# A scan-attention and gated-MLP kernel on one Trainium2 core: another start-up, and eight shared slots for raw weights and splits

## The chip, the cores and the metric

The kernel runs on one core of a Trainium2 chip. Five engines run side by side, each with its own instruction stream in order: TensorE (PE, matmuls from SBUF into PSUM), VectorE (DVE), ScalarE (ACT), GpSimd (POOL) and SyncE (SP, which here only issues DMAs). They meet through semaphores. The metric is the device time of one execution in microseconds; the median of several executions counts.

## The reference

Two stages. The first is a chunked linear recurrence over a sequence of 768 for 4 batches and 8 heads (head size 32, state size 16), the second a gated MLP over the 3072 resulting tokens (256 wide, 1536 hidden). Both are computed in float32.

```python
log_a = np.log(np.clip(a, 1e-06, 1.0))
for c in range(nc):
    ...
    cum = np.cumsum(la, axis=-1)
    L = np.exp(cum[:, :, :, None] - cum[:, :, None, :])
    L = L * causal
    CB = np.einsum('bhin,bhjn->bhij', Cc, Bc)
    y_intra = np.einsum('bhij,bhjd->bhid', CB * L, xc)
    y_inter = np.einsum('bhin,bhnd->bhid', Cc, state) * decay_to_i[:, :, :, None]
    ...
    state = decay_full[:, :, None, None] * state + np.sum(Bx, axis=2)

g = x @ w_gate
silu = g * (1.0 / (1.0 + np.exp(-g)))
return (silu * (x @ w_val) @ w_out).astype(np.float32)
```

## The kernel before

The sequence is cut into six blocks (`k` = 0 to 5) of 128 positions for all batches, and each block into two pieces of 64 (`Q`). A block goes through the attention stage and then through the MLP.

**Attention of a block.** The decays are running products of the clipped `a`. `L` holds, for each pair of positions, the product of the decays between them: DVE scans it (`scan_j`, one scan of 520 elements a batch) over a tile in which each row of `a` is repeated on 64 partitions, with `dj` (a repeated unit matrix) marking where each product starts. `E` holds the decays from a piece's start in the layout of the states, scanned with `dn`. The matmuls are `scores` (tile `S`, from `C` with the heads apart, `Cz`, and `B`), `sums` (tile `st`, the new states from x and the weighted B), `values` (tile `y`, from x and `L` after DVE's `mix` multiplied `S` into it) and `carried` (added into `y`, from `C` times `E` and the state `T`). `apart` masks `st` into `T`, on ACT or DVE; `step` carries the state from piece to piece. `weigh_b` (written into `xb`) and `weigh_c` (written into `bc`) apply the decays to B and C.

For blocks 1 to 5 the decays come from a clipped copy in DRAM: `all` is loaded (two DMAs), clipped by `clip_all` on DVE, and written to `clipped`; `load_aj` and `load_an` then read it with repetition over partitions. Block 0 has its own way in: for three batches (`SPREAD = 3`) eight rows of `a` (`rows`, clipped by `clip_rows`) are spread over 128 partitions by a matmul with a selection matrix `pick`, in two halves of 260 columns (tiles `a`), and scanned out of PSUM; the fourth batch and `E` are loaded with repetition by DMA, clipped and scanned in SBUF.

**MLP of a block.** For each of 12 slices `f` of the hidden size, `gate_val` computes gate and value (tiles `gv`, two matmul groups), `silu` (ACT) and `product` (DVE) give `sg`, `hid_high` and `hid_low` split `sg` into two float32r halves `hh` and `hl`, and `project` adds three float32r matmuls per output half into `po`. From block 1 on, gate and value are also three float32r products of split operands; block 0 uses float32 matmuls on x as it is (`xf`), since the split weights are not ready.

**Weights.** The 18 weight tiles (12 `wg`, 6 `wo`) are passed as 64-bit words, and each is fetched (`w_fetch`, 512 KB, tile `wg0r` and so on in pool `raw`) and brought to float32 in steps on ACT and DVE (`w_magnitude`, `w_range`, `w_rest`, `w_shift`, `w_sign`, `w_round`, the last shown as CUSTOM_DVE_ANT_0 on `wg0w`), then split (`w_high`, `w_low`). A raw slot is free after `w_round`. There are four.

**Order.** Nothing is issued where the code names it. Each step is added to a `Plan` (line 43) with its engines, an estimated cost, a rank (due time), what it needs, which slots it takes and what it uses; `Plan.order` (line 114) picks again and again the step that can start first, by rank, and so fixes each engine's stream. `Ordered` (line 184) keeps the streams in that order. A wait in a stream holds up all that stands behind it there. `idle` adds filler matmuls (tile `rest`, 128 columns of ones times 384) in two groups given by `IDLE` (line 851). `LATE` holds some loads back until a certain weight has been fetched.

Of the kernel before, what the change touches and what calls it, by code (L numbers as in the profile page):

```python
# [19 lines left out]
P = 128  # L20
# [10 lines left out]
HB = 4  # L31

# [10 lines left out]
class Plan:  # L43
# [49 lines left out]
    def chain(self, e, order):  # L93

        steps = {op.gives: op for op in self.ops if e in op.engines}
        for g, h in zip(order, order[1:]):
            steps[h].needs += (("issued", g),)
        for g, op in steps.items():
            if g not in order:
                op.needs += (("issued", order[-1]),)  # L100
        self.marked = {steps[g]: ("issued", g) for g in order}
# [12 lines left out]
    def order(self):  # L114
# [14 lines left out]
        while len(out) < len(self.ops):  # L129
# [31 lines left out]
            given = [(op.gives, end), (self.marked.get(op), self.clock[e])]  # L161
# [41 lines left out]
def scan_moe_kernel(ctx: ExitStack, tc, aj, an, bc, xb, wgv, wo, cst, sel, out):  # L203
# [13 lines left out]
    raw = pool("raw", 4)  # L217
# [23 lines left out]
    def load_rows():  # L241

        t = moe.tile([K * BATCH, 2, T + 32], F32, tag="xl", name="rows")
        t = bl[0]["rows"] = t[:, 0, : H * W]
        sp.dma_start(t, aj[0].rearrange("q (b c) -> (q b) c", b=BATCH))

    def load_first_aj():

        t, c = bl[0]["L"][:, H * SPREAD :], SPREAD * H * W
        for q in range(K):  # L250
            sp.dma_start(
                t[piece(q)].rearrange("p g t -> p (g t)"),
                aj[0, q, c:].unsqueeze(0).to_broadcast([Q, BATCH * H * W - c]),
            )

    def load_first_an():
        sp.dma_start(
            bl[0]["E"].rearrange("p b q t -> p (b q t)"),
            an[0].unsqueeze(1).to_broadcast([H, N, BATCH * K * W]),
        )  # L260
# [45 lines left out]
    def clip_all():  # L306
        clip(bl[0]["all"].rearrange("p i a t -> p (i a) t")[:, :, 1:])

    def clip_j(b):
        clip(bl[0]["L"][:, H * b : H * b + H, 1:])  # L310

    def clip_n():
        clip(bl[0]["E"].rearrange("p b q t -> p (b q) t")[:, :, 1:])
# [5 lines left out]
    def clip_rows():  # L319
        clip(bl[0]["rows"].rearrange("p (g t) -> p g t", t=W)[:, :, 1:])  # L320
# [334 lines left out]
    load_first_aj()  # L655
    load_first_an()
# [3 lines left out]
    def do(f, *a):  # L660
# [4 lines left out]
        dict(mm=4, at=4, L=1, E=1, bc=1, xb=1, Cz=1, T=2, raw=4, w=1, x=2, hh=HB, sg=SG, ob=2),  # L665
        dict(SP=3.0, Act=3.0, DVE=1.0, PE=1.5, Pool=2.0, Page=0.0, **{"-": 0.7}),
# [3 lines left out]
    GV, PO, ATT, FIRST, PACE0 = 2.82, 1.41, 5.0, 18.0, 3.5  # L670
# [16 lines left out]
    add("DVE", 0.6, lambda: ve.tensor_copy(dj, eye.unsqueeze(1).to_broadcast([P, H, W])), -8.5, ["cs"], gives="dj")  # L687
# [25 lines left out]

    add("SP", 0.96, load_all, -6, gives="all", lag=1.5)
    add("DVE", 0.3, clip_all, 3.0, ["all"], gives="clipped")
    add("SP", 0.48, write_all, -6, ["clipped"], gives="written", lag=1.5)


    for k in range(NB):
# [10 lines left out]
        q = ("SP", 0.48) if k else ("-", 0.0)  # L730

# [175 lines left out]
```

## Time and profile before

| what | us |
|---|---|
| median of 3 runs | 367.49 (365.65 to 367.71) |
| the profiled execution, its own time | 365.92 |
| its span, first to last instruction | 364.1 |
| PE busy / DVE busy / ACT busy | 354.8 / 233.4 / 127.2 |
| first gate/value matmul of block 0 | 23.20 |
| last output matmul done, the chain's end on PE | 360.9 |

A row of a timeline gives start, length, engine, line, operation, output and inputs (partitions x elements) and a count; neighbours of one kind are merged. In brackets stands the idle time ahead of the row and what ended it. A row of the chain of waits gives start, length and what the end of the program hung on during that time. A row of grouped DMA issues gives the count, the size of one and the time from issue to landing. "SPq" is SyncE's queue. All compute lines are L192, the helper that records every operation, so tiles tell the rows apart.

### The profile page before, as it was taken

To read this page: it belongs to the slowest core of one execution; us is meant where nothing else is said; L and a number is where in the kernel's file an instruction comes from. 1 tells how busy PE (TensorE), PEld (TensorE's weight loads), DVE (VectorE), ACT (ScalarE), POOL (GpSimd) and SP (SyncE) were. 2 spreads that over 40 slices of the span, in tenths; PEclk is the share of its full clock that TensorE was granted. 3 is DMA by queue.
4 is the path that set the end of the run, shared out by engine and by line. 5 is a ranking of instruction groups with operands and counts; after the bars stand their busy time and mean duration, and the time that the engine had idled before them with its cause. 6 is when DMAs were issued, how large, how long until landed. Compare 5 with 4: busy or idle time off the path is not lost.

```text
span 364.1 us, 7409 instructions
## 1 busy us (share of the span) xinstructions
PE 354.8 (97%) x3199; PEld 267.6 (73%) x3199; DVE 233.4 (64%) x430; ACT 127.2 (35%) x223; POOL 0.8 (0%) x6
## 2 busy tenths in 40 slices
PE   8989799999999999999999999999999999999996
PEld 4544345578886788878788878788888788888895
DVE  3997899998999579547166947158755153343250
ACT  3454674543423463322133322133221133321242
POOL 0000000000000000000000000000000000000000
PEclk9999999999999999999999999999999999999999
DMA  7669552484100065100048100036100000100001
GB/s 221 246 205 205 194 175 75 169 206 132 59 0 4 2 194 156 58 0 4 2 119 174 59 0 4 2 121 171 59 2 2 2 2 0 58 2 0 0 2 58
DMA packets 8736, 28.60 MB, mean 79 GB/s; under 512 B 1008, under 2 KB 1912, under 8 KB 8064
## 3 DMA queue, kind: packets, MB, share of 16 engines
q1 hardware_dynamic: 8416, 26.82, 25.2%
q10 hardware_dynamic: 288, 1.31, 0.9%
q8 instruction: 25, 0.41, 0.5%
q14 instruction: 7, 0.06, 0.0%
HBM read 24.79 MB, written 3.35 MB: 77 GB/s over the span
## 4 chain that ended last, share of the span: by engine, by line
PE 85%; DMA 5%; DVE 5%; ACT 1%; issue 1%; SPq 1%; DVEq 0%; ACTq 0%
PE gv L192 51%; PE po L192 27%; PE y L192 4%; DMA L<-clipped 4%; DMA L<-in_aj 2%; PE S L192 2%; DVE L L192 1%; PE rest L192 1%; PE st L192 1%; DVE sg L192 1%; SPq L192 1%; DVE wg0w L192 0%; DVE wo4w L192 0%; DVE wo3w L192 0%; ACT sg L192 0%
## 5 line engine op out<-in xcount | busy, mean ns | idle before, releaser
L192 DVE TENSOR_TENSOR sg<-gv,sg 128x512 f32<-128x512 f32 x72 | 49.5, 687 | 78.1 <-PE gv L192 77.9
L192 ACT ACTIVATE sg<-gv 128x512 f32<-128x512 f32 x72 | 43.0, 597 | 112.9 <-PE gv L192 112.8
L192 DVE TENSOR_TENSOR hl<-sg,hh 128x512 fp32r<-128x512 f32 x72 | 49.2, 688 | 22.2 <-ACT hh L192 21.6
L192 ACT CAST hh<-sg 128x512 fp32r<-128x512 f32 x54 | 33.6, 622 | 44.2 <-PE po L192 25.5
L192 DVE TENSOR_TENSOR_SCAN L<-L,dj 128x520 f32<-128x520 f32 x21 | 25.4, 1230 | 4.3 <-DMA L<-clipped 4.3
L192 DVE TENSOR_TENSOR L<-S,L 128x512 f32<-128x512 f32 x24 | 15.4, 682 | 1.9 <-PE S L192 1.9
L192 ACT COPY ob<-po 128x512 f32<-128x512 f32 (+1 forms) x13 | 7.2, 555 | 21.1 <-PE po L192 20.6
L192 PE MATMUL rest<-unit 128*128 128x384 bf16 x47 | 12.7, 421 | 1.1 <-DVE warm L192 1.1
L192 PEld LDWEIGHTS y<-L,xb 64*32 64x32 f32 x768 | 8.4, 105 | 4.7 <-issue 3.6
L192 PEld LDWEIGHTS <-unit 128*128 128x128 bf16 x47 | 5.3, 120 | 7.7 <-issue 5.7
L192 PE MATMUL y<-L,xb 64*32 64x64 f32 x768 | 10.4, 224 | 0.0
L192 PE MATMUL po<-hh,wo0h 128*128 128x512 f32 (+1 forms) x26 | 10.3, 395 | 0.0
L192 PE MATMUL po<-hh,wo2h 128*128 128x512 f32 (+1 forms) x26 | 9.8, 378 | 0.0
L192 PE MATMUL po<-hh,wo3h 128*128 128x512 f32 (+1 forms) x26 | 9.8, 377 | 0.0
L192 PE MATMUL po<-hh,wo5h 128*128 128x512 f32 (+1 forms) x26 | 9.8, 377 | 0.0
L192 PE MATMUL po<-hl,wo0h 128*128 128x512 f32 (+1 forms) x26 | 9.7, 375 | 0.0
L192 PE MATMUL po<-hh,wo0l 128*128 128x512 f32 (+1 forms) x26 | 9.7, 374 | 0.0
L192 PE MATMUL po<-hh,wo1h 128*128 128x512 f32 (+1 forms) x26 | 9.7, 373 | 0.0
L192 PE MATMUL po<-hl,wo2h 128*128 128x512 f32 (+1 forms) x26 | 9.7, 373 | 0.0
L192 PE MATMUL po<-hl,wo3h 128*128 128x512 f32 (+1 forms) x26 | 9.7, 373 | 0.0
L192 PE MATMUL po<-hh,wo4h 128*128 128x512 f32 (+1 forms) x26 | 9.7, 373 | 0.0
L192 PE MATMUL po<-hl,wo4h 128*128 128x512 f32 (+1 forms) x26 | 9.7, 373 | 0.0
(285 smaller groups left out, 778.9 us busy)
## 6 DMA issues: line engine op xcount, KB each, us to landing
L<-clipped SPq DMA_DIRECT2D x10, 520.0 KB
xb<-in_xb SPq DMA_DIRECT2D x5, 768.0 KB
out<-ob SPq DMA_DIRECT2D x11, 256.0 KB, 2.2
bc<-in_bc SPq DMA_DIRECT2D x5, 512.0 KB
E<-clipped SPq DMA_DIRECT2D x5, 260.0 KB
xb<-in_xb ACTq DMA_DIRECT2D x1, 768.0 KB, 5.9
bc<-in_bc ACTq DMA_DIRECT2D x1, 512.0 KB
wg0r<-in_wgv SPq DMA_DIRECT2D x1, 512.0 KB
```

The costliest lines, as they stand in the source:

```text
L192: ins = getattr(self.engine, name)(*a, **k)
```

## The change

What it does:

- All four batches of block 0's `L` and its `E` are spread by TensorE from `rows`, which now holds eight rows of `aj` and eight of `an`; `pick` has five selection matrices. `load_first_aj`, `load_first_an`, `clip_j` and `clip_n` are gone. `E` is scanned out of PSUM in two halves, by an order written out after the four mixes.
- `cs` is loaded first on ACT's queue; SP begins with the two loads of `rows` and `pick`, then the two of `all`. `dj` may be copied by ACT.
- `clip_all` runs on GpSimd and is ranked early. The weights wg2 to wg6 and block 1's `bc` and `xb` need `clipped` or `written`; the weights are fetched in their order.
- Pool `raw` has eight slots. `hh` and `hl` of a slice are halves of one tile from the same pool, where before each had four slots of its own.
- `chain`, which tied one engine to an order, becomes `follow`, which ties a list of steps whichever engine they run on; three lists are followed.
- `IDLE` has three groups of eight: at the start, after the scores of block 0, and after its carried values. `unit` is three times as wide, so that a filler reads it without repetition.
- Some estimated costs, lags and ranks of the planner change; `apart` of block 0 is given to ACT.

```diff
+RAW = 8
-    def chain(self, e, order):
-        steps = {op.gives: op for op in self.ops if e in op.engines}
+    def follow(self, order):
+        steps = {op.gives: op for op in self.ops}
         for g, h in zip(order, order[1:]):
             steps[h].needs += (("issued", g),)
...
-    raw = pool("raw", 4)
+    raw = pool("raw", RAW)
...
-    unit = const.tile([P, P], BF16, name="unit")
-    pick = const.tile([K * BATCH, SPREAD, P], F32, name="pick")
+    unit = const.tile([P, 3 * P], BF16, name="unit")
+    pick = const.tile([H, BATCH + 1, P], F32, name="pick")
...
     def load_rows():
-        t = moe.tile([K * BATCH, 2, T + 32], F32, tag="xl", name="rows")
-        t = bl[0]["rows"] = t[:, 0, : H * W]
-        sp.dma_start(t, aj[0].rearrange("q (b c) -> (q b) c", b=BATCH))
-    def load_first_aj():
...
-    def load_first_an():
...
+        t = moe.tile([H, 2, T + 32], F32, tag="xl", name="rows")
+        t = bl[0]["rows"] = t[:, :, : H * W]
+        sp.dma_start(t[:, 0], aj[0].rearrange("q (b c) -> (q b) c", b=BATCH))
+        sp.dma_start(t[:, 1], an[0])
...
     def clip_all():
-        clip(bl[0]["all"].rearrange("p i a t -> p (i a) t")[:, :, 1:])
+        t = bl[0]["all"].rearrange("p i a t -> p (i a) t")[:, :, 1:]
+        ge.tensor_scalar(t, t, 1e-6, 1.0, ALU.max, ALU.min)
...
     def scan_spread(b, i):
+        if b < BATCH:
+            to, d = bl[0]["L"][:, H * b : H * b + H].rearrange("p g t -> p (g t)"), dj
+        else:
+            to, d = bl[0]["E"].rearrange("p b q t -> p (b q t)"), dn
...
     def hid_high(k, f, e):
         t = hid[k, f]
-        for n in ("hh", "hl"):
-            t[n] = moe.tile([P, T], F32R, tag=n, name=f"{n}{k}_{f}", bufs=HB)
+        pair = raw.tile([P, 2, T], F32R, tag="wraw", name=f"hh{k}_{f}")
+        t["hh"], t["hl"] = pair[:, 0], pair[:, 1]
         copy(e, t["hh"], t["sg"])
...
     load_rows()
+    se.dma_start(cs, cst)
     sp.dma_start(pick, sel)
-    sp.dma_start(cs, cst)
...
-        add("SP", 0.48, do(w_fetch, i), r - 9.0, takes=[("raw", ("raw", i))], gives=("raw", i), lag=1.75)
+        add("SP", 0.48, do(w_fetch, i), r - 9.0, ["clipped"] if 2 <= i < 7 else [("y", 0)] if i == 7 else [], takes=[("raw", ("raw", i))], gives=("raw", i), lag=2.1)
...
-    add("SP", 0.96, load_all, -6, gives="all", lag=1.5)
-    add("DVE", 0.3, clip_all, 3.0, ["all"], gives="clipped")
-    add("SP", 0.48, write_all, -6, ["clipped"], gives="written", lag=1.5)
+    add("SP", 0.96, load_all, -9, gives="all", lag=0.9)
+    add("Pool", 1.0, clip_all, -9, ["all"], gives="clipped")
+    add("SP", 0.48, write_all, -9, ["clipped"], gives="written", lag=0.9)
...
+    halves = [(b, i) for b in range(BATCH) for i in range(2)]
+    plan.follow([
+        *(("spread", b, i) for b, i in halves), *(("S", 0, b) for b in range(BATCH)),
+        *(("spread", BATCH, i) for i in range(2)), *(("st", 0, b) for b in range(BATCH)), ("idle", 1, 0),
+    ])
+    plan.follow([("raw", i) for i in range(NW)])
+    plan.follow([("L", 0, b) if i else ("scan0", b) for b, i in halves] + [("M", 0, p) for p in range(NP)] + [("scan0", BATCH), ("E", 0), ("ce", 0)])
...
-SPREAD = 3
-IDLE = [-9.0] * 8 + [-3.8, -3.3, -2.8] + [-1.2 + 0.1 * i for i in range(12)], [15.0 + 0.5 * i for i in range(24)]
+IDLE = [-9.0] * 8, [-1.2 + 0.1 * i for i in range(8)], [0.5 + 0.5 * i for i in range(8)]
+IDLE_AFTER = [], [("S", 0, BATCH - 1)], [("y", 0)]
+FETCH = dict(aj=10.0, an=29.0, bc=12.0, xb=31.0)
```

The streams that come out of it, at three places. First SP, from the first weight on; names carry the block or weight number and then a buffer number. Before:

```order
L192 DMA wg0r_124<-in_wgv 128x1024
L192 DMA wg1r_129<-in_wgv 128x1024
L192 DMA wg2r_133<-in_wgv 128x1024
L192 DMA wg3r_140<-in_wgv 128x1024
L192 DMA clipped_85<-all_114 128x2x195
L192 DMA bc1_356<-in_bc 128x1024
L192 DMA xb1_366<-in_xb 128x1536
L192 DMA wg4r_381<-in_wgv 128x1024
L192 DMA L1_359<-clipped_85 64x2080 x2
L192 DMA E1_360<-clipped_85 128x1x520
L192 DMA wg5r_403<-in_wgv 128x1024
L192 DMA wg6r_418<-in_wgv 128x1024
```

And now, from the same weight on:

```order
L190 DMA wg0r_115<-in_wgv 128x1024
L190 DMA wg1r_121<-in_wgv 128x1024
L190 DMA clipped_85<-all_108 128x2x195
L190 DMA wg2r_210<-in_wgv 128x1024
L190 DMA wg3r_231<-in_wgv 128x1024
L190 DMA wg4r_233<-in_wgv 128x1024
L190 DMA wg5r_272<-in_wgv 128x1024
L190 DMA wg6r_275<-in_wgv 128x1024
L190 DMA bc1_363<-in_bc 128x1024
L190 DMA L1_365<-clipped_85 64x2080 x2
L190 DMA E1_366<-clipped_85 128x1x520
L190 DMA wg7r_390<-in_wgv 128x1024
```

The write of `clipped` moved ahead of wg2, and wg4 to wg6 moved ahead of all loads of block 1; `xb1` went behind wg7.

On PE, at the first gate/value tiles of block 0 (`gv0`, slice, gate or value), there stood before:

```order
L192 MATMUL gv0_0_0_383<-xf_119,wg0w_259 128x512 x2
L192 MATMUL gv0_0_1_400<-xf_119,wg0w_259 128x512 x2
L192 LDWEIGHTS unit_81
L192 MATMUL rest1_222<-unit_81 128x384
L192 MATMUL gv0_1_0_414<-xf_119,wg1w_290 128x512 x2
```

There stands now:

```order
L190 MATMUL rest2_361<-unit_81 128x384
L190 MATMUL gv0_0_0_382<-xf_123,wg0w_229 128x512 x2
L190 MATMUL gv0_0_1_401<-xf_123,wg0w_229 128x512 x2
L190 MATMUL gv0_1_0_417<-xf_123,wg1w_328 128x512 x2
L190 MATMUL gv0_1_1_429<-xf_123,wg1w_328 128x512 x2
```

The fillers between the tiles are gone; the last group of eight ends right ahead of the first tile. Ahead of the scores of block 0 stand eight spreads in a row, and behind them the two for `E`, then `st` and `y`, eight fillers and the carried values.

On DVE, from the last mix of `S` into `L` to the rounding of wg0 (`wg0w`) and the copies of `xf`, before:

```order
L192 TENSOR_TENSOR bc0_96<-bc0_96,E0_91 128x4x64
L192 TENSOR_TENSOR T0_105<-st0_0_197,cs_78 128x256
L192 TENSOR_TENSOR T0_105<-st0_1_198,cs_78 128x256
L192 TENSOR_SCALAR all_114<-all_114 128x6x64
L192 TENSOR_SCALAR wg0w_259<-wg0w_259 128x512
L192 TENSOR_SCALAR wg1w_290<-wg1w_290 128x512
L192 TENSOR_SCALAR wg0w_259<-wg0w_259 128x512
L192 TENSOR_SCALAR wg1w_290<-wg1w_290 128x512
L192 SCALAR_TENSOR_TENSOR wg0w_259<-wg0r_124,wg0w_259 128x512
L192 COPY xf_119<-y0_0_292 128x4x64
L192 COPY xf_119<-y0_1_293 128x4x64
L192 ISA wg0w_259<-wg0r_124,wg0w_259 128x1024
```

Now (a scan is shown as SCALAR_TENSOR_TENSOR, the rounding as ISA):

```order
L190 TENSOR_TENSOR L0_91<-S0_3_152,L0_91 128x4x2x64
L190 SCALAR_TENSOR_TENSOR E0_92<-a4_0_190,dn_80 128x260
L190 TENSOR_SCALAR wg0w_229<-wg0w_229 128x512
L190 SCALAR_TENSOR_TENSOR E0_92<-a4_1_194,dn_80 128x260
L190 TENSOR_SCALAR wg0w_229<-wg0w_229 128x512
L190 TENSOR_TENSOR bc0_97<-bc0_97,E0_92 128x4x64
L190 SCALAR_TENSOR_TENSOR wg0w_229<-wg0r_115,wg0w_229 128x512
L190 TENSOR_SCALAR wg1w_328<-wg1w_328 128x512
L190 ISA wg0w_229<-wg0r_115,wg0w_229 128x1024
L190 COPY xf_123<-y0_0_288 128x4x64
L190 COPY xf_123<-y0_1_289 128x4x64
```

The two masks of `T0` and the clip of `all` left DVE, the halves of `E`'s scan came behind the mixes, and the rounding of wg0 moved ahead of the copies of `xf`. GpSimd, which before held only memsets, now holds the clip of `all` behind them and behind one further instruction, shown as ISA.

More of the change, by code (lines that the diff above doesn't have):

```diff
@@ L91, in stay @@
         return more
-    def chain(self, e, order):
-        steps = {op.gives: op for op in self.ops if e in op.engines}
+    def follow(self, order):
+        steps = {op.gives: op for op in self.ops}
         for g, h in zip(order, order[1:]):
             steps[h].needs += (("issued", g),)
[L98 to L101, printed above, removed]
+        self.marked.update({steps[g]: ("issued", g) for g in order})
     def clocked(self, t, cost, rows):
@@ L160, in order @@
                 end = bus + 0.9
-            given = [(op.gives, end), (self.marked.get(op), self.clock[e])]
+            given = [(op.gives, end), (self.marked.get(op), self.clock[e] - self.SAME.get(e, 0.0))]
             for key, when in given:
@@ L640, in idle @@
         if not i:
-            rest[n] = ps_at.tile([P, 3, P], F32, tag="at", name=f"rest{n}")
-        te.matmul(rest[n], unit, unit.unsqueeze(1).to_broadcast([P, 3, P]), start=True, stop=True)
+            rest[n] = ps_at.tile([P, 3 * P], F32, tag="at", name=f"rest{n}")
+        te.matmul(rest[n], unit[:, :P], unit, start=True, stop=True)
     load_rows()
+    se.dma_start(cs, cst)
     sp.dma_start(pick, sel)
-    sp.dma_start(cs, cst)
     new_decays(0)
@@ L654, in scan_moe_kernel @@
     load_xb(0)
-    load_first_aj()
-    load_first_an()
     ge.memset(dn, 0.0)
@@ L737, in scan_moe_kernel @@
+        add(*q, load(load_xb), FETCH["xb"] if k == 1 else z - 6 if k else -6, late + behind("xb") + loaded, takes=[("xb", XB)], gives=("xb", k), lag=3.1)
         if not k:
             add("-", 0.0, lambda: None, -9, takes=[("x", "rows")], gives="rows", lag=0.2)
-            add("DVE", 0.35, clip_rows, -9, ["rows"], gives="clip")
-            add("-", 0.0, lambda: None, -7.5, [("decays", 0)], gives="aj", lag=2.4 * (BATCH - SPREAD) / 2)
-            add("-", 0.0, lambda: None, -7, [("decays", 0)], gives="an", lag=1.3)
@@ L742, in scan_moe_kernel @@
-            for b in range(BATCH):
-                r = z + 0.5 + b
-                for i in range(2 if b < SPREAD else 0):
+            for i in range(2):
+                add("DVE", 0.35, do(clip_rows, i), -9 + i, ["rows"], gives=("clip", i))
+            for b in range(BATCH + 1):
+                r = z + 0.5 + b if b < BATCH else -1.3
+                for i in range(2):
                     t = ("spread", b, i)
-                    add("PE", 0.45, do(spread, b, i), r + 0.5 * i, ["clip", "pick"], takes=[("at", t)], uses=[t, "rows"], gives=t, kind="s", rows=0.1)
+                    add("PE", 0.45, do(spread, b, i), r + 0.5 * i, [("clip", b // BATCH), "pick"], takes=[("at", t)], uses=[t, "rows"], gives=t, kind="s")
@@ L753, in scan_moe_kernel @@
[L753 to L756 removed]
+                    done = ("scan0", b) if not i else ("L", 0, b) if b < BATCH else ("E", 0)
+                    add("DVE", 0.63, do(scan_spread, b, i), r + 0.5 * i, need, uses=[t], gives=done)
+        else:
+            add("SP", 0.96, do(load_aj, k), FETCH["aj"] if k == 1 else z - 12, ["written", ("decays", k), *late], gives=("aj", k), lag=4.3)
+            add("SP", 0.48, do(load_an, k), FETCH["an"] if k == 1 else z - 9, ["written", ("decays", k), *late], gives=("an", k), lag=1.1)
```

67 lines of the change are left out of this document (23 added, 44 removed).

## The prediction

> **What bounds the kernel now.** I read the page's head and chain first, then the busy time by stage, then TensorE (PE) in order of time, and last the rows that a stalled PE waited for.
>
> ```profile
> span 364.1 us, 7409 instructions
> PE 85%; DMA 5%; DVE 5%; ACT 1%; issue 1%; SPq 1%; DVEq 0%; ACTq 0%
> 23.17:60.00 36.83, 34.11 (x209) 15.67 (x210) 33.86 (x71) 23.42 (x42) 0.00 (x0) 1.00 0.66 195
> 60.00:100.00 40.00, 40.00 (x330) 27.74 (x329) 36.98 (x66) 17.71 (x32) 0.00 (x0) 1.00 0.46 133
> 147.40:360.90 213.50, 213.49 (x1829) 174.73 (x1827) 107.42 (x189) 57.58 (x102) 0.00 (x0) 1.00 0.13 37
> ```
>
> The stage rows give start and end, length, then busy us of PE, its weight loads, DVE and ACT. PE does 213.49 of 213.50 us from 147.4 on, and all of 60 to 100. The change moves no matmul of that work, so only what lies before it can move the end.
>
> ```profile
> 23.20 3.67 PE L192 MATMUL gv<-xf,wg0w 128*128 128x512 f32 x8 [1.25 <-DVE wg0w L192]
> 30.46 1.14 PE L192 MATMUL rest<-unit 128*128 128x384 bf16 x6
> 35.52 3.60 PE L192 MATMUL gv<-xf,wg3w 128*128 128x512 f32 x8
> 38.96 3.60 PE L192 MATMUL gv<-xf,wg4w 128*128 128x512 f32 x8
> 45.25 3.67 PE L192 MATMUL gv<-xf,wg5w 128*128 128x512 f32 x8 [2.70 <-ACT wg7r L192]
> ```
>
> One gate/value tile of block 0 takes 38.96 - 35.52 = 3.44 us when nothing lies between. Five would take 17.20. From the first (23.20) to the sixth (45.25) PE took 22.05, so 4.85 us are lost: tile 3 starts 12.32 after tile 0 instead of 10.32, 2.00 of filler matmuls (`rest`, such as the six at 30.46); then 38.96 + 3.44 = 42.40 to 45.25 is 2.85 of waiting. The wait is named for ACT wg7r, but the tile needs wg5:
>
> ```profile
> 22.45 0.61 DVE wg0w L192
> 23.06 0.02 SPq L192
> 24.04 13.54 DMA L<-clipped
> 26.47 0.42 SPq L192 DMA_DIRECT2D wg5r<-in_wgv  x1
> wg5r<-in_wgv SPq DMA_DIRECT2D x1, 512.0 KB, 12.2
> 40.05 0.68 ACT L192 ACTIVATE wg5w<-wg5r 128x512 f32<-128x512 f32 x1
> 44.42 0.68 DVE L192 CUSTOM_DVE_ANT_0 wg5w<-wg5r,wg5w 128x1024 uint16<-128x1024 uint16 x1
> ```
>
> With four raw slots SP waits for DVE to finish wg0 (23.06) before it fetches wg4, block 1's L and wg5; L takes 13.54, wg5 12.2, landing at 38.7, and from ACT's first touch to the matmul it takes 45.25 - 40.05 = 5.20.
>
> **The change, part by part.** *Eight slots, order of fetches.* wg0 to wg6 now need no freed slot; wg2 to wg6 stand on SP behind GpSimd's clip and the write of the clipped decays, ahead of block 1's loads.
>
> ```profile
> 9.04 0.33 SPq L192 DMA_DIRECT2D wg3r<-in_wgv  x1
> wg3r<-in_wgv SPq DMA_DIRECT2D x1, 512.0 KB, 7.0
> 12.27 0.68 ACT L192 ACTIVATE wg0w<-wg0r 128x512 f32<-128x512 f32 x1 [4.50 <-DMA wg0r<-in_wgv]
> wg6r<-in_wgv SPq DMA_DIRECT2D x1, 512.0 KB, 12.6
> ```
>
> wg0 landed at 12.27, wg3 at 9.04 + 7.0 = 16.04: 1.26 us a weight. `all` is now fourth on SP, issued near 2; what is smaller than wg0 and ahead of it should land no slower than wg0's 5.9, and the clip end near 8. Five weights behind it land by about 16; tile 2's due time is 30. Block 1's bc and L leave once the carried matmuls of block 0 (about 22) let go of bc; even at the 13.54 of before L lands at 36.1, and its first user is DVE's scan ahead of `st` of block 1, which stands behind seven tiles (23.2 + 24.1 = 47.3). E and wg7 wait on SP for DVE's state step (near 25); wg7 at the slowest row, 12.6, lands at 38.6 and is due at 47.3 - 5.2 = 42.1. So the 2.85 go; what covers them is this spare of 3.5 us. After tile 4, DVE has 2.5 us of weight work and product per tile (0.34 + 0.34 + three at 0.60, the starts' spacing) against 3.44 of PE. Term: **-2.85**, between -2.85 and 0.
>
> *Fillers.* 24 instead of 47, none among the tiles: **-2.00**; they are PE time, so nothing hides them.
>
> *Start of tile 0: PE.*
>
> ```profile
> 1.05 2.74 PE L192 MATMUL rest<-unit 128*128 128x384 bf16 x8 [1.05 <-DVE warm L192]
> 3.93 2.94 PE L192 MATMUL a<-rows,pick 8*128 8x260 f32 x6
> 7.87 2.96 PE L192 MATMUL a<-rows,pick 8*128 8x260 f32 x6
> 10.76 2.01 PE L192 MATMUL S<-Cz,bc 32*64 32x128 f32 x64
> 13.44 4.08 PE L192 MATMUL rest<-unit 128*128 128x384 bf16 x13
> 17.45 0.80 PE L192 MATMUL y<-L,xb 64*32 64x64 f32 x60
> 18.59 0.84 PE L192 MATMUL y<-L,xb 64*32 64x64 f32 x60
> 19.36 0.69 PE L192 MATMUL y<-bc,T 32*64 32x64 f32 x32
> 19.99 1.96 PE L192 MATMUL rest<-unit 128*128 128x384 bf16 x11
> 54.98 1.21 PE L192 MATMUL S<-Cz,bc 32*64 32x128 f32 x64
> ```
>
> PE runs at two speeds that the granted clock (1.00 throughout) does not show. A filler takes 0.32 at first and 0.16 from 19.99; S 2.01, later 1.21 (ratio 1.66). The spreads (`a`, two rows each) cost 0.98 and stay slow although PE works without a break from 1.05 to 12.8. The fast speed comes only after 3.7 us of full-width fillers (13.44 to about 17.1).
>
> [...]
>
> Now eight spreads stand in a row: 3.93 + 8 x 0.98 = 11.8 (up to 0.3 more, since `unit` is three times as wide). S to 13.8, its issue to 13.4; two spreads for E (new, in place of E's DMA) 1.96 to 15.4; then st and y, 1.98 in before (17.45 to 19.43) at the fast speed, x 1.66 = 3.29 at the slow: 17.4 to 18.7. Eight fillers 1.43 to 2.56, carried 0.69 to 1.15, ACT's two xf copies 0.37 each, beside them eight fillers again. Fast from 15.4 on, tile 0 could start at 17.4 + 1.43 + 0.69 + 1.43 = 20.9; slow throughout, at 18.7 + 2.56 + 1.15 + 2.56 = 24.9. I take the middle: the speed rises in the first group of fillers, as it did once before after 3.7 us; 18.7 + 2.4 + 0.69 + 1.43 = 23.2.
>
> *Start of tile 0: DVE and ACT.*
>
> ```profile
> 15.83 1.28 DVE L192 TENSOR_TENSOR L<-S,L 128x512 f32<-128x512 f32 x2
> 18.82 0.76 DVE L192 TENSOR_TENSOR T<-st,cs 128x256 f32<-128x256 f32 x2 [1.38 <-PE st L192]
> 21.70 0.75 DVE L192 COPY xf<-y 128x256 f32<-128x256 f32 x2
> 22.37 0.68 DVE L192 CUSTOM_DVE_ANT_0 wg0w<-wg0r,wg0w 128x1024 uint16<-128x1024 uint16 x1
> 53.16 0.62 ACT L192 ACTIVATE T<-st,cs 128x128 f32<-128x128 f32 x2 [0.25 <-PE st L192]
> ```
>
> In before DVE idles 1.38 for st, masks T, clips `all`, and rounds wg0 at 22.97. Now T is ACT's (two pairs of 0.62, 1.24 beside PE's fillers), `all` GpSimd's, dj ACT's. S again sets the first mix near 14; two of the three xb in its midst are done before, so the mixes end near 16.7 (17.1 - 0.4). Then E in two halves 1.20, wg0's range and shift 0.68, bc 0.35, sign 0.60, wg1's range 0.34, round 0.60: 20.5; xf 0.67: 21.1. So DVE, which set 23.20, no longer does; PE's chain is late next. Term for the start: **0**, between -2.1 (DVE's 21.1) and +1.7 (24.9).
>
> *The rest.* Clipping E's and L's big tiles goes; the rows' second clip stands beside landing DMAs. Merging hh and hl into one of eight tiles gives more slots where PE is already full: 0. Constants first: 0, since `pick`, third on SP, lands behind the first fillers (in before its user started 3.93, right after them).
>
> Sum against the profiled execution (365.92, with 1.8 around its span): 365.92 - 2.85 - 2.00 + 0 = 361.07. The median of the runs shown is 367.49; the three runs and the profiled one average 366.7, 0.8 above the profiled one, so I forecast 361.07 + 0.8 = **361.9**.
>
> **Rivals.**
> - *A, slow start.* PE stays slow to the end of the fillers: tile 0 at 24.9 (+1.7), and its first quarter still slow (0.86 us of work takes twice that): 361.9 + 1.7 + 0.86 = 364.5. For: 8-row and narrow matmuls did not raise it in 11.7 us. Against: two groups of eight fillers, 2.56 each, nearly touch. 0.17.
> - *B, fast start.* [...] I put 359.1, 0.12: the slow spreads speak against it.
> - *C, GpSimd's clip is late (the slower side).* wg2 to wg6, then L, E and wg7, queue on SP behind it. GpSimd's rows are all memsets; one more instruction stands ahead of the clip there with no row to price it. DVE's own clip was short:
>
> ```profile
> 0.73 0.70 POOL L192 MEMSET dn<- 128x520 f32 x2 [0.29 <-POOLq L896]
> 19.49 0.35 DVE L192 TENSOR_SCALAR all<-all 128x384 f32<-128x384 f32 x1
> ```
>
>   Tile 2 is due at 23.2 + 6.9 = 30.1, less 5.2 of work, less 3 for a fetch on a free queue: the clip must end by about 21.5. Each us after that costs one: the gain is gone at 26.4, 1% is lost at 30.8 (371.2). From a landing near 7 that is over 20 us for what took DVE 0.35; I price an end at 27, 367.4. 0.06. [...]
> - *D, DVE becomes the bound.* It was 36.98 busy of 40 from 60 to 100; the same work must fit 4.85 us sooner. If it gives back half, 364.3. For: the packed stage. Against: PE never waited for it there. 0.09.
>
> **How the numbers follow.** Forecast 0.56 (tile 0 between 22 and 24.3: 360.7 to 363.0), A 0.17, B 0.12, C 0.06, D 0.09. The range 358.8 to 365.6 leaves out C and B's far end, about 0.1. 1% of 367.49 is 3.7 us, about what a measurement here can tell: under 363.8 lie the forecast, B and a little of D, less a little: faster 0.66; A, D and the rest of the middle 0.29; slower 0.05, C.
>
> **What would show it.** Right: no `rest` between gv tiles, tiles 0 to 6 spaced 3.44, no wait for wg5, wg5 landed by 18, tile 0 at 22 to 24.3. Wrong: the first st or y still slow at 18 and fillers of 0.32 right ahead of tile 0 (A); fillers of 0.16 after y (B); POOL's clip ending past 21 and PE waiting at tile 2 (C); PE waits named for DVE after tile 7 (D).

## The result, and the profile after

| | us |
|---|---|
| after, median of 20 runs | 363.53 (357.62 to 366.70) |
| before, median of 20 runs beside it | 365.72 (364.51 to 369.81) |
| ratio of after to before, 95% interval | 0.987 (0.983 to 0.991) |
| after and before once more, in the series of e9 | 363.64 and 365.51, ratio 0.996 (0.993 to 0.998) |
| profiled execution of after, its own time / its span | 362.51 / 360.7 (before 365.92 / 364.1) |

The change makes the kernel faster by about 2 us (363.53 - 365.72 = -2.2, and 363.64 - 365.51 = -1.9). The first ratio looks larger because it is taken from fast runs alone, and two of the 20 executions, at 357.62 and 360.01, lie so low that most of the others count as slow beside them; so I go by the medians, and e2 below shows what these two most likely are. The forecast was 361.9, so the change brought less than half of the 4.85 us that it was to bring; the profiled execution shows 3.4 (364.1 - 360.7).

These are the lines of after's page that answer to those shown of before: span, then the shares of the chain that ended last.

```profile
span 360.7 us, 7359 instructions
PE 90%; DVE 7%; issue 2%; DMA 1%; SPq 0%; ACT 0%; DVEq 0%; ACTq 0%
```

Next, what PE waited for in after: line waited for, total us, times, longest.

```profile
PE y L190 <- issue: 1.8, 1, 1.8
PE a L190 <- DMA pick<-in_sel: 0.8, 1, 0.8
PE gv L190 <- DVE wg9w L190: 0.7, 1, 0.7
```

The 2.70 ahead of wg5's tile and the 1.25 ahead of wg0's are gone. In their place stand a wait for `pick`, one ahead of `y` that the profile can name no releaser for ("issue"), and one for DVE at tile 9. PE's timeline shows where (start, length, operation, count, and the idle time ahead in brackets):

```profile
4.84 7.27 PE L190 MATMUL a<-rows,pick 8*128 8x260 f32 x16 [0.78 <-DMA pick<-in_sel]
12.04 2.01 PE L190 MATMUL S<-Cz,bc 32*64 32x128 f32 x64
13.98 2.10 PE L190 MATMUL a<-rows,pick 8*128 8x260 f32 x4
16.01 0.95 PE L190 MATMUL st<-xb 64*32 64x64 f32 x47
...
17.73 0.33 PE L190 MATMUL st<-xb 64*32 64x64 f32 x2
19.82 1.17 PE L190 MATMUL y<-L,xb 64*32 64x64 f32 x63 [1.76 <-issue]
20.92 2.26 PE L190 MATMUL rest<-unit 128*128 128x384 bf16 x8
23.11 0.69 PE L190 MATMUL y<-bc,T 32*64 32x64 f32 x32
23.74 1.47 PE L190 MATMUL rest<-unit 128*128 128x384 bf16 x8
25.05 3.60 PE L190 MATMUL gv<-xf,wg0w 128*128 128x512 f32 x8
28.48 3.60 PE L190 MATMUL gv<-xf,wg1w 128*128 128x512 f32 x8
...
42.21 3.60 PE L190 MATMUL gv<-xf,wg5w 128*128 128x512 f32 x8
45.65 3.60 PE L190 MATMUL gv<-xf,wg6w 128*128 128x512 f32 x8
...
59.91 2.38 PE L190 MATMUL gv<-xf,wg9w 128*128 128x512 f32 x5 [0.69 <-DVE wg9w L190]
```

Tile 5 starts 17.16 after tile 0, where before took 22.05: that is 4.89 less, and 4.85 was expected. But tile 0 starts at 25.05 instead of 23.20 (+1.85), so tile 5 comes 45.25 - 42.21 = 3.04 earlier. The wait for wg9 takes 0.7 of that back (tile 9: 62.26 - 59.91 = 2.35). Later 1.05 is won, of which 0.7 is a wait of before's that after does not have (for the state T, ahead of block 2's S); the other 0.3 I have not placed. 2.35 + 1.05 = 3.4, the difference of the spans.

So one question carried the experiments: what is the 1.76 of "issue" ahead of y's second half? Its inputs were long ready (DVE's last mix ended at 16.8). After's page also counts the packets of a queue of the kind "instruction" (queue, kind, packets, MB, share):

```profile
q8 instruction: 25, 0.41, 0.4%
```

Two theories:

- *F, PE waits for its own program.* The 25 packets have 16 KB each. The page counts 6368 matmuls and weight loads for PE (3184 of each), and 6368 / 25 = 255, so by this estimate a packet would hold some 255 of PE's instructions. In the trace's list of DMA packets, from which all packet times here come, the first one of after starts at 17.35 and takes 1.05.
- *W, it waits for a signal.* DVE's sign step on wg0 ends at 19.58, 0.24 ahead of y; a wait that is counted on DVE's stream could hang on it.

### The profile page after: what moved, and what is told of

The parts are those of the page before. It is cut to its first block, busy times and chain, and to the rows that moved or that the text cites. A ratio compares the mean times of both kernels' runs of the same rounds, so it can differ in the third digit from the quotient of the medians.

```text
span 360.7 us, 7359 instructions
## 1 busy us (share of the span) xinstructions
PE 353.0 (98%) x3184; PEld 268.8 (75%) x3184; DVE 238.6 (66%) x446; ACT 115.7 (32%) x209; POOL 2.3 (1%) x7
## 3 DMA queue, kind: packets, MB, share of 16 engines
HBM read 24.28 MB, written 3.35 MB: 77 GB/s over the span
## 4 chain that ended last, share of the span: by engine, by line
PE 90%; DVE 7%; issue 2%; DMA 1%; SPq 0%; ACT 0%; DVEq 0%; ACTq 0%
PE gv L190 51%; PE po L190 28%; PE y L190 4%; PE a L190 3%; PE S L190 2%; DVE L L190 1%; PE st L190 1%; DVE sg L190 1%; PE rest L190 1%; DMA pick<-in_sel 1%; DVE wg9w L190 1%; DVE wg7w L190 1%; DVE wg8w L190 1%; DVE T L190 1%; DVE wg5w L190 0%
## 5 line engine op out<-in xcount | busy, mean ns | idle before, releaser
L190 DVE TENSOR_TENSOR hh<-sg,hh 128x512 fp32r<-128x512 f32 x72 | 49.4, 692 | 12.1 <-ACT hh L190 10.7
L190 ACT CAST hh<-sg 128x512 fp32r<-128x512 f32 x39 | 24.1, 622 | 37.1 <-PE po L190 15.2
L190 PE MATMUL po<-hh,wo4h 128*128 128x512 f32 (+1 forms) x52 | 15.1, 373 | 0.0
L190 DVE CAST hh<-sg 128x512 fp32r<-128x512 f32 x33 | 14.1, 428 | 1.0
L190 PEld LDWEIGHTS po<-hh,wo4h 128*128 128x128 f32 x52 | 9.5, 188 | 1.7
L190 PEld LDWEIGHTS po<-hh,wo1h 128*128 128x128 f32 x52 | 9.5, 188 | 1.7
L190 PEld LDWEIGHTS po<-hh,wo2h 128*128 128x128 f32 x52 | 9.4, 188 | 1.8
L190 PEld LDWEIGHTS po<-hh,wo3h 128*128 128x128 f32 x52 | 9.4, 188 | 1.8
L190 PEld LDWEIGHTS po<-hh,wo5h 128*128 128x128 f32 x52 | 9.4, 188 | 1.7
L190 PEld LDWEIGHTS po<-hh,wo0h 128*128 128x128 f32 x52 | 9.2, 188 | 2.0 <-issue 0.2
```

The lines of the kernel that those rows point to most:

```text
L190: ins = getattr(self.engine, name)(*a, **k)
```

## The experiments

Each is an edit of after, except e7 and e8, which edit before. Medians stand beside that of before on the same chip in the same series (e1 to e4, e5 to e8, e9 to e12).

| run | edit | median, us | before, us | ratio (95%) |
|---|---|---|---|---|
| e1 | 32 tiny matmuls early on PE | 362.94 | 365.85 | 0.992 (0.988 to 0.995) |
| e2 | pick loaded first | 362.34 | 365.85 | 0.988 (0.982 to 0.994) |
| e3 | no fillers but the first eight | 363.50 | 365.85 | 0.988 (0.983 to 0.993) |
| e4 | e1 and e2 | 362.90 | 365.85 | 0.993 (0.990 to 0.996) |
| e5 | second fillers ahead of st and y | 361.33 | 366.31 | 0.985 (0.981 to 0.989) |
| e6 | wg4 to wg6 fetched late | 361.54 | 366.31 | 0.987 (0.982 to 0.992) |
| e7 | before, without 24 fillers | 365.38 | 366.31 | 0.998 (0.994 to 1.001) |
| e8 | before, eight slots, without 24 fillers | 366.98 | 366.31 | 1.002 (0.998 to 1.005) |
| e9 | after, unchanged | 363.64 | 365.51 | 0.996 (0.993 to 0.998) |
| e10 | clip of all on DVE | 364.70 | 365.51 | 0.996 (0.993 to 1.000) |
| e11 | e6 again | 361.60 | 365.51 | 0.991 (0.988 to 0.994) |
| e12 | e2, e5 and e6 together | 360.73 | 365.51 | 0.988 (0.983 to 0.992) |

Where two of these kernels are compared, I use the medians.

### e1 and e4: more instructions ahead of the stall

```diff
         te.matmul(rest[n], unit[:, :P], unit, start=True, stop=True)
+        for _ in range(32 if (n, i) == (0, 7) else 0):
+            te.matmul(rest[n][:32, :1], unit[:32, :32], unit[:32, :1], start=True, stop=True)
```

> After with 32 tiny matmuls (32 rows by 32, one column; a weight load and a matmul each) put behind the first eight fillers, where PE stands 0.78 us for pick; they fill an unused bank and nothing else is changed. Theory F: the 1.76 us in which PE stands ahead of y's second half (18.06 to 19.82) is PE waiting for its own program, fetched in pieces of 256 instructions (a 16 KB packet on the instruction queue starts at 17.35 and takes 1.05); 64 instructions more ahead move that fetch to about 14, so y's second half follows the first at once, near 18.1, tile 0 starts near 23.3 instead of 25.05, and the median falls by 1.0 to 1.8 against after. Theory W: the wait is for a signal of DVE (its sign step on wg0 ends at 19.58); then y's second half stays at 19.8, tile 0 at 25.0 to 25.3 and the time at that of after within 0.3.

> Both: pick first on SP and the 32 tiny matmuls behind the first fillers. If the stall is the fetch of PE's program (F) and pick's lateness goes right through (P), tile 0 starts at 22.5 to 23.0, about where it was forecast (23.2), and the median falls by 2.0 to 2.5 against after, less what DVE gives back at tile 9 (0.7 in after, up to 2 more). If F is wrong it is as with pick alone.

Where PE stands is fixed by the number of instructions behind it, not by the work. The row of busy time from the start to the end of the stall counts PE's matmuls and weight loads (the x behind the first two busy times); first after, then e4, then e1.

```profile
0.00:19.80 19.80, 15.96 (x221) 10.84 (x222) 12.78 (x26) 6.39 (x13) 2.34 (x7) 1.00 0.77 279
```

```profile
0.00:19.05 19.05, 16.42 (x221) 11.34 (x222) 12.13 (x26) 4.66 (x7) 2.34 (x7) 1.00 0.81 276
```

```profile
0.00:20.25 20.25, 18.03 (x349) 11.84 (x349) 13.42 (x29) 7.77 (x15) 2.34 (x7) 0.75 0.79 272
```

In e4 PE stops after the same 221 matmuls as in after, though 32 of them are new, and so in the midst of y's first half (1.34 from 17.7 on), where no signal is due. In e1 it passes that place and stops 128 matmuls and 127 weight loads further on, one packet later: 0.97 in the middle of the carried matmuls. The same 221 return in e6, e9 and e10. In each case work goes on 2.25 to 2.47 after the packet's start (after: 19.82 - 17.35; e4: 19.09 - 16.76; e1: 20.32 - 18.07). W is refuted and F holds. One part of the expectation failed: the 64 instructions did not bring the packet to about 14 in e4 (16.76), so reaching a place in the program is not all that sets its start (e10 and e11 below). Nor did the time come: both medians are only some 0.6 below after's, where 1.0 to 1.8 and 2.0 to 2.5 were expected. In e4 the tiny matmuls last until 5.0, so its first spread starts at 4.93 and pick's gain is not in it; tile 0 starts at 25.61.

### e2: pick first

```diff
+    sp.dma_start(pick, sel)
     load_rows()
     se.dma_start(cs, cst)
-    sp.dma_start(pick, sel)
```

> After with pick's load issued first on SP instead of third. Theory P: the 0.78 us wait for pick ahead of the first spread is a loss that goes right through to tile 0; pick lands near 0.74 + 3.2 = 3.9 or a little later, the first spread starts at 4.1 to 4.3, every step up to tile 0 comes 0.5 to 0.75 earlier (24.3 to 24.5), and so does the end. Rival: the rows, now second and third, land 0.3 to 0.5 later with their clip behind them, and the first spread stays at 4.6 to 4.9; no change.

The first spread starts at 3.99, directly behind the fillers, instead of 4.84 (and 5.05 in e9, 5.56 in e10: pick's landing varies). So the rival (4.6 to 4.9) falls. The median is 1.2 below after's, with overlapping intervals. Whether pick's gain goes through to tile 0, as theory P has it, this profile can't tell, because its execution is of another kind, as its rows show (for the stages start and end, length, busy time of PE, weight loads, DVE, ACT, POOL, then the granted clock):

```profile
3.99 5.02 PE L190 MATMUL a<-rows,pick 8*128 8x260 f32 x16
```

```profile
1.30:4.00 2.70, 2.68 (x9) 1.05 (x9) 0.41 (x1) 1.96 (x3) 0.11 (x1) 1.00 0.69 205
4.00:7.30 3.30, 3.30 (x14) 2.16 (x14) 2.43 (x5) 1.25 (x2) 0.00 (x0) 1.00 0.82 260
7.30:17.00 9.70, 9.70 (x268) 6.74 (x269) 8.50 (x19) 3.33 (x9) 1.49 (x1) 0.50 0.90 300
```

The first spreads come every 0.22, not 0.43, until about 7.3; from there to 17 the clock is granted at 0.50. So PE's speed did rise behind the eight first fillers in this execution (below: an early rise), for some 3.3 us (3.99 to about 7.3), and the spreads did not hold it. The rise brings more than faster spreads (5.02 for the 16 instead of 7.27): with PE further on, the first packet starts at 12.14, and y has no stall. Tile 0 starts at 20.01, 5.04 earlier than in after; 2.25 by the spreads, 1.76 by the stall and 0.85 by the earlier first spread are most of that. This execution took 357.19, the other five 361.95 to 363.86. The two low executions of after are most likely of this kind (their mean granted clocks are 0.986 and 0.981, where the ordinary ones read 0.999 or 1.00), but they have no profile of their own.

### e3: without the fillers

```diff
-IDLE = [-9.0] * 8, [-1.2 + 0.1 * i for i in range(8)], [0.5 + 0.5 * i for i in range(8)]
+IDLE = [-9.0] * 8, [], []
```

> After without the eight fillers ahead of the carried matmuls and the eight ahead of tile 0 (the eight at the start stay). [...] Rival: PE's speed rises without them (by busy time of any kind), tile 0 takes 3.44, and 2.0 to 3.0 us are gained. [...]

The median, 363.50, is that of after: the 16 fillers cost what they bring. The profile shows how; PE's timeline of e3:

```profile
18.53 5.19 PE L190 MATMUL gv<-xf,wg0w 128*128 128x512 f32 x8 [0.82 <-ACT xf L190]
23.56 3.60 PE L190 MATMUL gv<-xf,wg1w 128*128 128x512 f32 x8
```

Tile 1 follows tile 0 after 5.03, not after the rival's 3.44 (3.43 in after): without fillers ahead of it, 1.60 goes into a slow tile 0. This too is an execution with an early rise, so its starts don't compare with after's.

### e5: the fillers where they hide the fetch

```diff
-        *(("spread", BATCH, i) for i in range(2)), *(("st", 0, b) for b in range(BATCH)), ("idle", 1, 0),
+        *(("spread", BATCH, i) for i in range(2)), ("idle", 1, 0), ("idle", 1, 7), *(("st", 0, b) for b in range(BATCH)),
```

> After with its second group of eight fillers put ahead of block 0's st and y, where before had its thirteen, instead of behind y. The group's 16 instructions last 1.3 to 2.6 us, so PE's program has time to arrive: theory F says no stall inside or between st and y (the boundary that stopped PE after 449 counted instructions in after is reached only near 20, when the piece fetched from 17.35 on is there). Tile 0 then starts near 22.8 if the fillers raise the speed ahead of st and y (as in before), near 25.3 if st and y stay slow; without F (theory W, a wait for DVE) PE stands again until 19.8 or later ahead of y's second half. Median 361.3 to 363.7 against 363.5 of after.

The same number of matmuls, the same fillers, another place: the median is 361.33, 5.0 below its before, where after is 2 below. In the profile (an execution with an early rise, like e2's) the first packet starts at 16.15, yet st and y run without a break, from 17.11 to 19.55, and tile 0 starts at 21.78. The eight fillers now stand where before had its thirteen. Those most likely covered the fetch there unseen, though no run takes them out: before's first packet starts at 14.73, when PE has fillers to run until 17.45.

### e6, e10 and e11: what makes the packet late

Edit of e6 and e11, and of e10:

```diff
-        add("SP", 0.48, do(w_fetch, i), r - 9.0, ["clipped"] if 2 <= i < 7 else [("y", 0)] if i == 7 else [], takes=[("raw", ("raw", i))], gives=("raw", i), lag=2.1)
+        add("SP", 0.48, do(w_fetch, i), r - 9.0, ["clipped"] if i == 2 else [("y", 0)] if 3 <= i < 8 else [], takes=[("raw", ("raw", i))], gives=("raw", i), lag=2.1)
...
+    plan.follow([("raw", 6), ("bc", 1)])
```

```diff
-        ge.tensor_scalar(t, t, 1e-6, 1.0, ALU.max, ALU.min)
+        clip(t)
...
-    add("Pool", 1.0, clip_all, -9, ["all"], gives="clipped")
+    add("DVE", 0.35, clip_all, -9, ["all"], gives="clipped")
```

> After with wg4, wg5 and wg6 issued behind block 1's L, so that SP holds them until the carried matmuls are done (about 21) and the DMA engines are quiet from about 14 to 21. Theory Q: the piece of PE's program that came late in after (packet at 17.35, with the DMA engines busy 0.86 to 1.04 of the time from 7 to 18) stood behind the weights that the change moved up; with quiet engines its packet starts within 1.5 us of the S matmuls' end (by 15.6), and the stall of 1.76 falls to under 0.5, tile 0 near 23.3 to 23.8. Theory L: the fetch has a fixed latency from its own trigger; packet again at 17.0 to 17.6, stall 1.5 or more, tile 0 at 25. The later weights may cost a wait at tile 4 to 6 (wg4 lands near 33, due near 33.5), so the time itself is no test: 361.5 to 365.

> The kernel of e6_quiet once more, since its profiled execution was one with a fast start. Theory Q (the late piece of PE's program stood behind the weights): in an execution with a slow start the packet starts by 15.6 and the stall falls under 0.5, tile 0 near 23.5, 1.2 to 2.2 less than after. Theory L (it did not): packet near 17, stall of 1.5 or more after the same 449 counted instructions; the gain on after then needs another place, and I would look for it ahead of tile 9, where after waited 0.7 for DVE.

> After with the clip of all back on DVE; the planner puts it behind seven of the eight scans of L (near 11.5), so the clipped decays' write and wg2 to wg6 leave SP from about 12 instead of 7.7. Theory N (GpSimd's clip buys nothing in after, eight slots are enough): wg2 lands by 20, wg6 by 26, both ahead of what tile 2 (31.9) and tile 6 (45.6) need 5.2 us earlier; tile 0 comes at most 0.35 later, time equal to after within 0.4. Rival G: the 4.4 us later fetches end in a wait ahead of tile 2 or 3, or block 1's L behind them ends in one ahead of its y; 0.5 to 3 us slower.

The rows of busy time from 14 to 20 end with the share of time in which the DMA engines were busy and with GB/s. After, e11, e10:

```profile
14.00:17.00 3.00, 3.00 (x86) 2.13 (x82) 2.89 (x6) 0.00 (x0) 0.00 (x0) 1.00 1.02 418
17.00:20.00 3.00, 1.24 (x96) 1.07 (x89) 2.77 (x7) 1.92 (x6) 0.00 (x0) 1.00 0.17 60
```

```profile
14.00:17.00 3.00, 3.00 (x84) 2.13 (x86) 2.98 (x6) 0.00 (x0) 0.00 (x0) 1.00 0.50 190
17.00:20.00 3.00, 3.00 (x138) 2.31 (x124) 2.75 (x7) 2.01 (x6) 0.00 (x0) 1.00 0.02 7
```

```profile
14.00:17.00 3.00, 3.00 (x60) 1.80 (x52) 2.33 (x6) 0.00 (x0) 0.00 (x0) 1.00 0.95 217
17.00:20.00 3.00, 1.78 (x129) 1.61 (x114) 3.00 (x7) 1.20 (x5) 0.00 (x0) 1.00 0.97 339
```

And PE's timeline at y's second half, e11 and then e10:

```profile
17.81 1.17 PE L190 MATMUL y<-L,xb 64*32 64x64 f32 x63
...
23.25 3.60 PE L190 MATMUL gv<-xf,wg0w 128*128 128x512 f32 x8
```

```profile
21.91 1.17 PE L190 MATMUL y<-L,xb 64*32 64x64 f32 x63 [3.14 <-issue]
...
28.54 3.60 PE L190 MATMUL gv<-xf,wg0w 128*128 128x512 f32 x8
```

After has the engines full until 17 and its packet at 17.35. With wg4 to wg6 held back (e11) they empty between 15 and 16, the packet starts at 15.48, the stall is gone, and tile 0 starts at 23.25. With the same weights sent later (e10, wg2 issued at 13.41) the packet starts at 19.46 and the stall grows to 3.14. The counts say the same. In no trace does the first packet start before PE has begun 181 of its matmuls and weight loads (181 in e3, 183 in e2, 184 in e11 and e12), about one packet ahead of the 443 at which it stops. PE begins the 181st at 14.48 in e11, 14.58 in after and 15.29 in e10, and the packet follows 1.0, 2.8 and 4.2 later; in e4 it is 12.92 and 3.8. So in these runs the place in the program sets how early the packet can start, and the load on the DMA engines how late it does; a fixed latency (L) is refuted, and theory Q holds: the piece of PE's program stands behind the weights. e6 fits once its DMAs are read instead of its schedule: `all` landed so late that wg2 left at 11.04, the weights ended at about 16.9, the packet started at 16.91 and the stall was 2.50, so its expectation (engines quiet from 14) was wrong in its premise. What exactly holds the packet, the transfers' order on one engine or the reading of the queue, no run tells.

e10 also prices GpSimd's part. Its median is 1.06 above e9's (364.70 - 363.64), more than theory N allows (0.4), though the two ratios' intervals overlap. G has the size but not the place: tiles 0 to 6 stand 3.43 apart in e10, and what its profile loses to e9's lies ahead of tile 0 (28.54 against 26.57), where the stall is 1.37 longer than e9's 1.77 and pick happened to land 0.5 later. That profile is of e10's longest execution (366.66), so it shows the place better than the price. Clipping early on GpSimd most likely pays because it moves the weights out of the way of PE's program.

### e7 and e8: the two terms on before

```diff
-IDLE = [-9.0] * 8 + [-3.8, -3.3, -2.8] + [-1.2 + 0.1 * i for i in range(12)], [15.0 + 0.5 * i for i in range(24)]
+IDLE = [-9.0] * 8 + [-3.8, -3.3, -2.8] + [-1.2 + 0.1 * i for i in range(12)], []
```

e8 has this and the eight shared slots (`raw` of 8; `hh` and `hl` as one tile of it).

> Before without the 24 fillers that stood from block 0's carried matmuls to its tile 3. My prediction priced them at 2.00 of PE time that nothing hides. Theory X (they were hidden): tile 5 waits for wg5, whose landing (38.7) and preparation do not depend on PE, so PE reaches the same wait 2.0 earlier and waits 4.85 instead of 2.85; gain 0 to 0.3. Theory Y (sum of terms): 2.0 gained, wait for wg5 still 2.85. The first tiles may run slow, since eleven of the 24 stood ahead of tile 0: that would cost up to 1.7 at the start, which X hides too.

> Before with the eight shared slots (raw weights and splits in one pool) and without the 24 fillers, the rest as it was: three batches spread, cs and E by DMA, clip of all on DVE. Theory Z (slots and fillers are the whole gain): the tiles 0 to 6 stand 3.44 apart and some 4.5 us are gained (361.2), unless block 1's L, which the order of SP now puts behind wg11, comes late; then st or S of block 1 moves back and PE waits ahead of block 1's y, and up to all of it is given back. Theory V (the order of fetches matters, not the slots alone): a wait of 2 us or more for L, E or block 1's first gv tiles, time 363 to 366.

PE's timeline of e7:

```profile
23.11 5.37 PE L192 MATMUL gv<-xf,wg0w 128*128 128x512 f32 x8 [3.14 <-DVE wg0w L192]
28.31 3.60 PE L192 MATMUL gv<-xf,wg1w 128*128 128x512 f32 x8
...
42.95 3.67 PE L192 MATMUL gv<-xf,wg5w 128*128 128x512 f32 x8 [0.73 <-DVE wg5w L192]
```

Without fillers ahead of it PE stands for 3.14, the granted clock is 0.50 from 24.34 to 27.75, and tile 0 takes 5.20 instead of 3.43, which gives 1.77 of the 2.0 back. (e7's and e8's profiles have an early rise too, but tile 0 waits for DVE's rounding of wg0 in both, as in before, and starts where it did.) Yet tile 5 comes 2.30 earlier than in before, because its wait falls from 2.70 to 0.73: wg5's preparation can't have been set by its landing alone, as X had it; what DVE does for the tiles ahead probably sets it too. Tile 9 then waits 1.09 for wg9, and the median is 0.9 lower, within the interval of no change. X and Y are both wrong in their reason.

In e8 tile 0 takes 5.21 again, tiles 1 to 8 stand 3.43 apart, tile 6 starts 3.18 ahead of before's, and nothing is gained (366.98 against 366.31). The place is block 1:

```profile
72.36 0.50 PE L192 MATMUL gv<-xh,wg0h 128*128 128x512 f32 x1 [0.63 <-ACT xh L192]
74.18 0.47 PE L192 MATMUL gv<-xh,wg0h 128*128 128x512 f32 x1 [1.31 <-DVE xh L192]
```

Block 1's L leaves SP at 32.07, behind wg11 (after: 24.36, ahead of it), and DVE scans it from 48.94 on (after: 39.96). So block 1's carried matmuls come behind block 0's last tile instead of ahead of it (after: 67.93, then tile 11), and nothing covers the making of xh. Between 72.36 and block 1's second slice e8 falls from 2.2 ahead of before to 1.0 behind: the two waits make 1.94 of it, and behind them the granted clock is 0.50 from 75.41 to 78.83. That is V's outcome in the time, though the waits are shorter than its 2 us: slots and missing fillers do not reach the end without the order of the fetches.

### e9 and e12: the base, and a better version

> After once more, unchanged, as the base for the other three on the same chip. Theory S: PE's early speed differs between executions of one program; where the first fillers (1.3 to 4.1) end in the fast speed, it lasts about 3.4 us, the spreads take some 2.5 us less and the time is near 358 to 360; else it is 362 to 365. So one to three executions in ten near 358 to 360, the rest at 362 to 365, median 363 to 364. Rival: the low times of after were another chip's or a mistake of one run, and all lie within 362 to 365.

> Three edits on after together: the second group of fillers ahead of st and y (e5), pick first (e2), wg4 to wg6 behind block 1's L (e6). If their gains on after (medians, each against before: 2.8, 1.2 and 2.6 us) were independent it would be 357; they are not, since the first two both take the stall away and pick only shifts what then waits for T and for DVE: I expect 359.5 to 361.5, 2 to 4 less than after, tile 0 at 21.5 to 22.5 and no stall of PE's program ahead of it. It is refuted as a better version if it is at 362.5 or more.

e9's twelve lie at 361.66 to 364.98, with the same stall (1.77) and wait for wg9 (0.68): S's low executions did not show here, and the rival's range nearly holds (362 to 365), though the three lowest (361.66, 362.45, 362.70) are again the only ones with a mean clock under 0.99. S rests on the profiles of e1, e2, e3, e5 and e6, all taken in executions whose first spreads were fast (the 16 in 4.53 to 5.30, against 7.26 to 7.30 in after, e4 and e9 to e12); e6's shows that such a start need not end in a low time, since its stall of 2.50 gave the gain back. In e9's profile (363.62, next to the median) the second group of fillers, behind y, is slow to its end, and tile 0 starts at 26.57.

e12 is the fastest: 360.73, against 363.64 for after and 365.51 for before in the same series; its interval there (0.983 to 0.992) does not touch after's (0.993 to 0.998), though it does that of the first comparison of after (0.983 to 0.991), which its two low executions pulled down. From e11 (361.60, 0.988 to 0.994) the runs do not tell it apart. PE's timeline:

```profile
3.99 7.30 PE L190 MATMUL a<-rows,pick 8*128 8x260 f32 x16
11.22 2.01 PE L190 MATMUL S<-Cz,bc 32*64 32x128 f32 x64
13.16 2.10 PE L190 MATMUL a<-rows,pick 8*128 8x260 f32 x4
15.19 2.74 PE L190 MATMUL rest<-unit 128*128 128x384 bf16 x8
17.86 1.17 PE L190 MATMUL y<-L,xb 64*32 64x64 f32 x63
...
22.66 3.70 PE L190 MATMUL gv<-xf,wg0w 128*128 128x512 f32 x8
```

Nothing stalls ahead of tile 0, which starts at 22.66, 2.39 earlier than in after and a little later than expected. Of what is left, PE waits 0.4 for wg4, 0.2 for wg7 and again 0.8 for T ahead of block 2's S, as before did: part of the start's gain returns there.

## Why the prediction was right and wrong

- *Wait for wg5, -2.85: right.* No wait up to tile 6; wg5 was issued at 9.70 and took 7.9, landed at 17.6 (said: by 18). The working had all five weights there by about 16; wg6, issued at 10.57, took 9.8, and the full DMA engines that this shows are what held the packet below. e8 shows the condition on which the term rests: the tiles' pitch alone is worth nothing where block 1's operands come late.
- *Fillers among the tiles, -2.00: right as a term*, since eight stayed ahead of tile 0. e7 shows what they were worth where none stay: 1.77 comes back in a slow tile 0.
- *Start of tile 0, 0 (between -2.1 and +1.7): this step failed;* it measured +1.85, beyond its bound. The working added PE's steps from 3.93 to 23.2 and had none for PE's own program. Without the 1.76, tile 0 of after would start at 25.05 - 1.76 = 23.29, and in e11, where the stall is gone, it starts at 23.25. The other parts nearly cancel: the first spread came at 4.84 (+0.9), the spreads at 0.90 for two instead of 0.98 (-0.6 for eight pairs), DVE had wg0 at 20.84 (said 20.5), so PE's chain was late next, as said. The fillers' speed rose in the group behind y, as said, after 1.6 us of it (0.32 apart from 20.92 to 22.50, 0.17 behind). That was one case of two: in e9, whose time is next to the median, it rose only in the last group, and tile 0 came 3.37 later than in before, by the stall of 1.77 and, for most of the rest, by fillers and carried matmuls at the slow speed.
- *The rest, 0: two errors that nearly cancel.* "Constants first: 0" was wrong: pick, issued at 1.54, took 3.17 and held PE for 0.78. Tile 9 waited 0.69 for DVE. Against that, before's wait of 0.7 for T was gone.
- *Rival A (slow start, 364.5)* has tile 0 at 24.9, and 25.05 was measured, but that is luck: in the profiled execution the fillers ahead of tile 0 were at full speed, and the stall made up the difference. e9 had A's mechanism on top of the stall, with tile 0 at 26.57, though not A's slow first quarter of tile 0 (3.43).
- *Rival B (fast start)* put 359.1, a time that single executions reach (after's lowest is 357.62). No run shows the term under it and under B's far end, 8-row spreads that raise the speed by themselves: in after all 16 stay 0.43 to 0.57 apart (7.27 in all), and in e2 they come every 0.22 from 3.99, directly behind the first eight fillers, and slow down again near 7.3 with PE busy. The stall was missing in that execution.
- *Rival C (late clip): refuted.* GpSimd's clip took four times as long as DVE's, but ended at 7.71:

```profile
6.22 1.49 POOL L190 TENSOR_SCALAR all<-all 128x384 f32<-128x384 f32 x1 [4.79 <-DMA all<-in_an]
```

- *Rival D (DVE gives it back): seen in small,* 0.7 at tile 9 instead of half of 4.85, at the place named.

The sum by measured terms: -2.85 - 2.00 + 1.85 + 0.7 - 1.05 = -3.35, against 3.4 between the spans. The time came out only 1.6 above the forecast though the gain is some 2.7 short, and that is luck: the forecast counted from 366.7, and before measured 365.72 beside after. With the program in time most of the gain is there: e11 has 361.60, 3.9 below its before, with 0.6 of new waits for wg4 and wg7 in the place of the 0.7 for wg9.

## What to carry to other kernels

Where an engine stands for "issue" with all its inputs ready, count its instructions up to there and look at the packets of the instruction queue: here the place stayed at 443 counted instructions when the work was shifted (after, e4, e6, e9, e10), and that was PE waiting for its program. St and y's first half, 64 narrow matmuls each with their weight loads, used up 2 x 128 = 256 instructions in some 2 us ahead of the stall (16.01 to 18.06 in after), so put slow, wide work (or nothing urgent) behind the point where a piece is fetched, and keep bulk loads off that time; loads moved forward to remove one wait can delay the program and cause another (the 1.76 of after, gone in e11). When a change removes fillers, ask for each whether it paid the speed of the next tile, covered a fetch, or only cost time: here the same eight matmuls left after some 2 us below before in one place, and 5.0 below it in another.

## What the runs showed of the hardware that I had not expected

- *PE can run out of program.* Stalls of 0.97 to 3.14 us at fixed instruction counts, 443 (after, e4, e6, e9, e10) and 698 (e1), 255 apart as the profile counts them, ended 2.25 to 2.47 after a 16 KB packet's start. PE's work did not hide the fetch: 64 of y's narrow matmuls with their weight loads pass in 1.1 us (after, 19.82 to 20.92), so by my estimate 255 instructions of this kind last 2.2, no longer than the 2.25 to 2.47 from a packet's start until work goes on.
- *Such a packet waits behind ordinary loads:* it started at 15.48, 17.35 and 19.46 as the weights were moved, 1.0, 2.8 and 4.2 after PE had begun its 181st counted instruction.
- *PE's early speed differs between executions of one program.* e6 and e11 are one kernel, and its first 16 spreads took 5.30 in the one and 7.27 in the other. With the same eight fillers ahead (1.32 to 4.06) the speed rose in e2 and stayed low in after. In e2 it fell again near 7.3, with PE busy throughout on 8-row matmuls, and in all seven traces with an early rise (e1, e2, e3, e5 to e8) the granted clock averages 0.51 to 0.67 up to 10 (from 7.3 in e1 to e3, from 7 in e5 to e8) and reads 0.50 from 10 to 14. What sets the time of the fall no run tells. The granted clock in the profile reads 1.00 until the first change on record, so it hid the slow start of after (1.00 throughout, though its fillers stood 0.32 apart up to 22.50 and 0.17 behind) and showed it in e2 (0.50 from 7.3).
- *GpSimd's clip of 128x384 took 1.49, DVE's 0.35.*
